# Rerouting the last small output rows of an attention-and-MLP backward kernel away from one DMA engine

## The chip, the cores and the metric

One Trainium2 chip, one core of it. The metric is the device time of one execution in microseconds (us); the profile's own span, from the first to the last instruction of the program, is 1.7 to 1.8 us shorter. The profile counts sixteen DMA engines for the core. A DMA engine takes its packets from several queues: those of the engine that ends last come from q0, q1 and q10 in the trace.

## The reference, cut to what matters

One token goes through a layer norm, attention over a cache of 32 heads x 8192 positions x 128, and a gated MLP. Asked for are the output and the gradients of eight inputs. Almost all of the bytes are the two caches (read once) and their two gradients (written once), each 64 MiB.

```python
def _f(A_x, A_k_cache, A_v_cache, A_wq, A_wo, B_w1, B_w3, B_w2):
    xn = _layernorm(A_x)
    return A_x + attention(xn, A_k_cache, A_v_cache, A_wq, A_wo) + swiglu(xn, B_w1, B_w3, B_w2)
_out, _vjp = jax.vjp(_f, ...)
return (_out, *_vjp(grad_out))   # out_0: 640 values; out_1, the gradient of x: 640 values; out_2, out_3: caches; ...
```

## The kernel before

Each head's keys and values are loaded as tiles of 128 partitions x 16 KiB, overwritten by their gradients, and stored from the same tiles. After the last head come the last weight gradients, then out_0 and out_1.

```python
def store(kind, h):
    t = kv_tiles.pop((kind, h))
    ...
    fifo((dkc if kind == "K" else dvc)[h], t[:])       # SP queue, 2 MB
    free_slots.append(t)
    load_next()
# ... cut: 32 heads ...
outers_a(H - 1)                                        # last V gradient and its store
outers_b(H - 1)                                        # last K gradient and its store
fin_od(NG - 1); fin_pe(NG - 1)
fin_wo(NG - 1)                                         # weight gradient, stored by POOL's queue
for ci in range(NC):
    fin_wq(NG - 1, ci)                                 # the same, after the fifth
# ... cut ...
nc.vector.tensor_copy(row_bf, acc[:, 0:DHALF])
out_0v = out_0.rearrange("a b (e c) -> (a b e) c", e=2)
for e in range(2):
    nc.scalar.dma_start(out_0v[e:e + 1, :], row_bf[64 * e:64 * e + 1, :])
# ... cut: backward of the layer norm, a chain of small operations ...
nc.vector.tensor_copy(fin_bf[:], ps_o[0:NC, 0:P])      # NC = 5 rows of 128
nc.scalar.dma_start(out_1.rearrange("a b (c p) -> (a b c) p", p=P), fin_bf[:])
```

## Time and profile before

| | before |
|---|---|
| median of the first three runs | 732.62 us (732.50 to 733.53) |
| span of the profiled run | 731.1 us |
| moved by DMA | 303.53 MB, mean 415 GB/s |
| last arithmetic ends, span ends | 717.2 us, 731.1 us |
| out_1's last landing, the last kv store's last landing | 722.19 us, 730.10 us |

Two things are to be read here: the DMA engines are full nearly throughout, and the end is 13.9 us in which no compute engine works. The lines that show both stand in the prediction. The queue that carries ACT's transfers, on the page of the kernel before (columns: packets, MB, share of sixteen engines):

```profile
q10 hardware_dynamic: 18, 0.01, 0.0%
```

Eighteen packets are five transfers: each row is one data packet and one semaphore packet, so the two input rows and two out_0 rows make 8, out_1 with its five rows makes 10.

### The profile page before, as it was taken

Reading aid. Unit: us, or ns where it says so; the run is one execution under the profiler, and the core shown is the slowest. Engines: PE = TensorE matmul, PEld = TensorE weight load, DVE = VectorE, ACT = ScalarE, POOL = GpSimd, SP = SyncE. Lnnn points to the kernel's source line nnn. Section 1 sums busy time; section 2 is a strip of 40 time slices with the busy share of each in tenths; the row PEclk is TensorE's granted clock in tenths of the full one; section 3 lists DMA queues with packets and bytes.
Section 4 is the critical chain, followed back from the end, with each engine's and each line's share of the span. In section 5 each row is a group of like instructions: output and inputs, shape, how many; then the busy total and the mean of one; then the engine's idle time right before and its main releaser. Section 6 shows DMA issues by size and latency. Waiting matters only on the chain.

```text
span 731.1 us, 12909 instructions
## 1 busy us (share of the span) xinstructions
PE 602.7 (82%) x5193; PEld 376.1 (51%) x5193; DVE 461.3 (63%) x811; ACT 375.8 (51%) x727; POOL 29.9 (4%) x45
## 2 busy tenths in 40 slices
PE   3989589999999989886987898789697879977930
PEld 2557356665566556554555554455464545544510
DVE  4179646677768886676546765647656775667581
ACT  3640736665666566554554554545464545555510
POOL 0010100000100000001000000000000000000000
PEclk9996799999999999999998999989999999999965
DMA  8999999999999999999999999999999999999993
GB/s 344 403 410 422 424 429 426 418 421 424 422 407 428 428 425 424 425 428 431 423 430 425 431 424 428 427 430 426 426 428 427 430 425 429 429 429 430 430 407 130
DMA packets 27135, 303.53 MB, mean 415 GB/s; under 512 B 2798, under 2 KB 4146, under 8 KB 10434
## 3 DMA queue, kind: packets, MB, share of 16 engines
q1 hardware_dynamic: 21328, 276.39, 89.4%
q0 software_dynamic: 5728, 26.30, 8.9%
q8 instruction: 41, 0.67, 0.4%
q14 instruction: 20, 0.16, 0.1%
q10 hardware_dynamic: 18, 0.01, 0.0%
HBM read 151.34 MB, written 151.34 MB: 414 GB/s over the span
## 4 chain that ended last, share of the span: by engine, by line
DMA 51%; PE 35%; DVE 6%; ACT 3%; issue 1%; SPq 0%; ACTq 0%; DVEq 0%
DMA kv<-in_A_k_cache_dram 22%; DMA out_dram<-kv 17%; PE pT L318 16%; DMA kv<-in_A_v_cache_dram 11%; PE sA L339 4%; PE dA L339 3%; PE X L433 3%; DVE kv L466 3%; PE m L356 2%; DMA wo_g<-in_A_wo_dram 2%; ACT KT L320 1%; ACT kv L630 1%; PE gu_ps L549 1%; PE dh_ps L560 1%; PE dx_acc L648 1%
## 5 line engine op out<-in xcount | busy, mean ns | idle before, releaser
L320 ACT COPY KT<-pT 128x512 f32<-128x512 f32 x512 | 288.0, 587 | 229.5 <-PE pT L318 209.0
L318 PE MATMUL pT<-ident_f,kv 128*128 128x128 f32 x2048 | 308.2, 290 | 60.3 <-DMA kv<-in_A_v_cache_dram 29.5
L318 PEld LDWEIGHTS pT<-ident_f,kv 128*128 128x128 f32 x2048 | 237.1, 149 | 153.7 <-issue 52.2
L466 DVE TENSOR_TENSOR kv<-qd,U 128x4096 bf16<-128x4096 bf16 x64 | 146.1, 2285 | 0.0
L466 DVE TENSOR_TENSOR kv<-qd,P 128x4096 bf16<-128x4096 bf16 x64 | 143.6, 2285 | 0.0
L433 PE MATMUL X<-kv,Z 128*32 128x512 bf16 x1024 | 94.3, 405 | 1.8 <-DVE Z L450 1.8
L339 PE MATMUL sA<-KT,qz 128*32 128x512 bf16 x512 | 83.9, 408 | 0.0
L339 PE MATMUL dA<-KT,qz 128*32 128x512 bf16 x512 | 83.8, 406 | 0.0
L416 DVE SCALAR_TENSOR_TENSOR U<-m,P 128x64 bf16<-128x64 f32 x32 | 7.5, 234 | 82.0 <-PE m L356 82.0
L382 DVE TENSOR_REDUCE mrow<-m 128x1 f32<-128x64 f32 x32 | 7.2, 223 | 75.3 <-PE m L356 75.2
L339 PEld LDWEIGHTS <-qz 128*32 128x32 bf16 x1024 | 29.5, 95 | 40.9 <-issue 38.3
L433 PEld LDWEIGHTS <-Z 128*32 128x32 bf16 x1024 | 32.5, 99 | 34.5 <-issue 6.9
L356 PE MATMUL m<-selc,KT 64*128 64x64 f32 x256 | 30.2, 240 | 8.1 <-ACT KT L346 7.9
L356 PEld LDWEIGHTS m<-selc,KT 64*128 64x128 f32 x256 | 21.3, 142 | 30.1 <-ACT KT L346 21.2
L376 ACT CAST qd<-pT 128x256 bf16<-128x256 f32 x32 | 11.9, 372 | 41.1 <-DVE kv L466 31.6
L389 DVE TENSOR_REDUCE negM<-m 128x1 f32<-128x128 f32 x32 | 9.3, 292 | 33.3 <-PE m L386 33.3
L514 DVE SCALAR_TENSOR_TENSOR wq_g<-wq_g,side 128x512 bf16<-128x512 bf16 x40 | 27.3, 683 | 0.0
L257 DVE SCALAR_TENSOR_TENSOR side<-wo_g,g_bc 128x640 bf16<-128x640 bf16 x32 | 26.2, 820 | 1.1 <-DMA wo_g<-in_A_wo_dram 0.7
L448 DVE SCALAR_TENSOR_TENSOR U<-m,P 128x128 bf16<-128x128 f32 x32 | 11.4, 355 | 15.7 <-PE m L446 15.7
L406 DVE RECIPROCAL rZ<-m 128x1 f32<-128x1 f32 x32 | 5.3, 167 | 24.1 <-PE m L400 24.1
L346 ACT COPY KT<-dA 64x512 f32<-64x512 f32 x32 | 18.6, 583 | 3.1 <-PE dA L339 3.1
L346 ACT COPY KT<-sA 64x512 f32<-64x512 f32 x32 | 18.6, 580 | 2.3 <-PE sA L339 1.9
(161 smaller groups left out, 373.3 us busy)
## 6 DMA issues: line engine op xcount, KB each, us to landing
out_dram<-kv SPq DMA_DIRECT2D x64, 2048.0 KB, 31.0
kv<-in_A_k_cache_dram SPq DMA_DIRECT2D x32, 2048.0 KB, 26.3
kv<-in_A_v_cache_dram SPq DMA_DIRECT2D x32, 2048.0 KB, 26.3
out_dram<-wo_g POOLq DMA_DIRECT2D x8, 640.0 KB, 11.5
out_dram<-wq_g POOLq DMA_DIRECT2D x8, 640.0 KB, 13.3
wq_g<-in_A_wq_dram POOLq DMA_DIRECT2D x7, 640.0 KB, 13.3
wo_g<-in_A_wo_dram POOLq DMA_DIRECT2D x7, 640.0 KB, 19.1
kv<-in_B_w_dram SPq DMA_DIRECT2D x2, 1728.0 KB, 27.9
```

What stands on the lines that cost most here:

```text
L257: nc.vector.scalar_tensor_tensor(junk[:], G_["wo"][:, hh, :], 1.0, g_bc[:], ALU.mult, ALU.mult, accum_out=G_["do"][:, hh:hh + 1])
L318: nc.tensor.transpose(pT[:, k * P:(k + 1) * P], W3[:, 4 * c + k, :], ident_f[:])
L320: nc.scalar.copy(KT[:].rearrange("p k w -> p (k w)"), pT[:])
L339: nc.tensor.matmul(S_[kind][q:q + QW, :], lhsT=S_["qz"][:, o:o + QW], rhs=KTb[c][:, par, :], start=(c0 == 0 and par == 0), stop=(c0 == NCH ...
L346: nc.scalar.copy(XS[0:QH].rearrange("p k w -> p (k w)"), S_.pop(kind)[0:QH, :])
L356: nc.tensor.matmul(S_["m"][:, b0:b0 + 4 * J].rearrange("p (x c k t) -> p k x c t", x=4, k=4, t=2)[:, k], lhsT=XS[0:QH, k, :], rhs=selc[0:Q ...
L376: nc.scalar.copy(qd[:].rearrange("p a d -> p (a d)"), hd[h].pop("ps_r"))
L389: nc.vector.tensor_reduce(S_["negM"][:], S_["m"][:, 2 * J:2 * J + P], AX.X, ALU.max, negate=True)
L433: nc.tensor.matmul(xg["X"][q:q + QW, :], lhsT=Z[:, o:o + QW], rhs=W[:, N4 * i:N4 * (i + 1)], start=(slot == 0 and i < 4), stop=(slot == NS ...
L448: nc.vector.scalar_tensor_tensor(S_["U2"][:], S_["V"][:, 0:J].unsqueeze(2).to_broadcast([P, J, 2]), S_["m"][:, OC + NS:OC + NS + 1], S_["P ...
L466: nc.vector.tensor_tensor(dst[:, lo * DH:hi * DH].rearrange("p (j a b) -> p j a b", a=DH // 2, b=2), vec.rearrange("p (a b) -> p a b", b=2 ...
L514: nc.vector.scalar_tensor_tensor(wq_g[:, ci, :], wq_g[:, ci, :], 1.0, dqb, ALU.mult, ALU.mult, accum_out=dxa[:, ci, g:g + 1])
```

## The change

The intent: DMA engine 4 finishes last, so no late small transfer should need it. Out_0 is to leave in four pieces for each half, out_1 as four rows and one row, all on engines 0 to 3.

```diff
-    out_0v = out_0.rearrange("a b (e c) -> (a b e) c", e=2)
+    out_0v = out_0.rearrange("a b (e q c) -> (a b e) q c", e=2, q=4)
     for e in range(2):
-        nc.scalar.dma_start(out_0v[e:e + 1, :], row_bf[64 * e:64 * e + 1, :])
+        nc.scalar.dma_start(out_0v[e:e + 1], row_bf[64 * e:64 * e + 1, :].rearrange("p (q c) -> p q c", q=4))
 ...
-    nc.scalar.dma_start(out_1.rearrange("a b (c p) -> (a b c) p", p=P), fin_bf[:])
+    for lo, hi in ((0, 4), (4, NC)):
+        nc.scalar.dma_start(out_1.rearrange("a b (c p) -> (a b c) p", p=P)[lo:hi, :], fin_bf[lo:hi, :])
```

## The prediction

> **What bounds the kernel now.** I read the page first: engines, slices, DMA queues, the chain that ended last.
>
> ```profile
> PE 602.7 (82%) x5193; PEld 376.1 (51%) x5193; DVE 461.3 (63%) x811; ACT 375.8 (51%) x727; POOL 29.9 (4%) x45
> ...
> DMA  8999999999999999999999999999999999999993
> GB/s 344 403 410 422 424 429 426 418 421 424 422 407 428 428 425 424 425 428 431 423 430 425 431 424 428 427 430 426 426 428 427 430 425 429 429 429 430 430 407 130
> ...
> DMA 51%; PE 35%; DVE 6%; ACT 3%; issue 1%; SPq 0%; ACTq 0%; DVEq 0%
> ```
>
> No compute engine is full; the DMA engines are at nine tenths or more in every slice but the first and the last, and half of the chain is transfers. The kernel is bound by moving 303.53 MB. The change touches only what happens after the last attention head, so the last slices matter: that slice (18 us) moves only 130 GB/s. Next, the timeline near the end:
>
> ```profile
> 714.85 0.26 ACTq L837 DMA_DIRECT2D out_dram<-KT  x1
> ...
> 716.93 0.28 DVE L853 CAST fin_bf<-pT 5x128 bf16<-5x128 f32 x1 [0.56 <-PE pT L851]
> 717.24 0.27 ACTq L854 DMA_DIRECT2D out_dram<-fin_bf  x1
> ```
>
> "KT" is the row of out_0, "fin_bf" the five rows of out_1. All arithmetic is done at 717.2, yet the span is 731.1. What fills the 13.9 us? The table of stretches (columns: busy time of PE, PEld, DVE, ACT, POOL, then clock, DMA share, GB/s):
>
> ```profile
> 718.00:721.00 3.00, 0.00 (x0) 0.00 (x0) 0.00 (x0) 0.00 (x0) 0.00 (x0) 0.50 0.31 124
> 721.00:730.00 9.00, 0.00 (x0) 0.00 (x0) 0.00 (x0) 0.00 (x0) 0.00 (x0) 0.50 0.06 25
> 730.00:731.10 1.10, 0.00 (x0) 0.00 (x0) 0.00 (x0) 0.00 (x0) 0.00 (x0) 0.50 0.00 0
> ```
>
> For nine microseconds the DMA share is 0.06, one sixteenth: **one** of sixteen DMA engines works alone, at 25 GB/s, and everything waits for it. The packet records of the trace name its work: packets of 16384 B on q1 (the big kv stores issued by SP, 611 to 614 ns each) alternating with 4096 B packets on q0 (the weight-gradient store issued by POOL, 160 ns), each starting as the one before ends, until 729.70. The waits of SP's queue say who is waiting:
>
> ```profile
> SPq L880 <- DMA out_dram<-wq_g: 12.0, 1, 12.0
> SPq L880 <- DMA out_dram<-KT: 9.1, 1, 9.1
> ...
> SPq L880 <- DMA out_dram<-kv: 2.2, 1, 2.2
> ```
>
> L880 is the wait for everything at the program's end. It waits 12.0 us, nominally for wq_g (landed 727.67 in the semaphore records), then for the last kv store (landed 730.10). The 9.1 us on "KT" ends at 716.8, long before.
>
> The landing records also say this is no accident of the end. The sixteenth landing of an SP transfer comes about 0.1 us after the fifteenth until 60 us into the run, 2 to 3 us after it near 300 us, and 11.0 us for the last store (719.07 and 730.10). One engine falls steadily behind. Is it the one that the change avoids? Out_1's five rows answer. Their 256 B packets ran at 717.99, 718.02, 718.07, 718.29 and **720.94**; the fifth sits inside the late engine's unbroken sequence (q1 packet 720.327 to 720.941, this packet 720.937 to 720.955, q0 packet from 720.951). So the late engine is the one carrying a single row of out_1, and I take it to be engine 4.
>
> **What the Trainium skill says.** (1) "DMA: Bandwidth & Descriptors", section "Why a DMA increments its semaphore by 16 and not by 1": a hardware-generated transfer uses the largest k up to 16 that divides both sides' slowest dimension, on the lowest-numbered k engines, and the unused 16 - k counts come at once. The trace agrees on counts: out_1's semaphore moves six times (one early step, five landings; k = 5), each out_0 transfer's twice (k = 1). So out_1 uses engines 0 to 4, and out_0 never used engine 4 before the change. (2) Same page, "Queues, rings and completion order": each engine goes round-robin between its queues, packet by packet. The q1/q0 alternation is that; an added small packet takes its own duration and displaces nothing else. (3) Same page, "Anatomy of one DMA": a completion waits for the write's receipt. Here the last packet ends at 729.70 and the semaphore moves at 730.10, 0.40 us, which the change leaves alone. (4) "Runtime: NRT & Kernel Launch", section "Instruction fetch mechanics": instructions arrive in 16 KiB blocks of 256. Queue q8 shows 41 such packets; PE has 10,386 counted instructions, and 10,386 / 256 = 40.6. I suspect those fetches make one engine late; the change does not touch them.
>
> **The change part by part.**
> *Out_1, fifth row off engine 4.* Removes one 256 B packet and its semaphore write from the late engine. Net cost there, start to next start: 720.937 to 720.951 is 14 ns, 721.717 to 721.723 is 6 ns. Gain: 0.02 us, on the path that sets the end.
> *Out_1, second transfer.* One more issue on ACT, 0.27 us (the L854 row), so about 717.5. It lands by about 719 on an engine that is idle: the four early rows ran within 1.1 us of the issue. The end is at 730.1, so some 11 us of slack hide it.
> *Out_0 in four pieces.* Data and semaphore packets go from 4 to 16 in all, at 9 to 30 ns, spread over four engines and done near 716 to 717: nothing on the path.
> *Semaphores.* Transfers from SP and ACT take eight semaphores in turn (100, 102, 103, 104, 106, 108, 109, 110). The last stores have 104, 106, 108, and ACT's three have 100, 102, 103. A fourth ACT transfer may take 104 and push the stores to 106, 108, 109. Their earlier users landed at 697.45, 702.46 and 707.35, so issues may move from 695.87, 701.77, 706.17 to about 697.5, 702.5, 707.4: later by 0.7 to 1.6 us. But the fifteen faster engines still have older stores to drain then (until 703.1, 708.0 and 712.9), the late one longer still, so no engine runs dry. At the end SP walks its semaphores 59 to 65 ns apart; with the last store one place later in that walk, one step fewer follows it: a gain of 0.06 us.
> Sum: -0.02 -0.06 = -0.08 us, or -0.02 if the semaphores stay. 732.62 - 0.08 = 732.54; I say 732.5.
>
> **The rivals.**
> *Out_1 sets the end.* Then freeing it from the late engine's queue would pay. Its last landing was at 722.19, against about 718.9 for the other four: up to 3.3 us, giving 729.3. Against it: the kv store lands at 730.10, 7.9 us after out_1, from the same engine. Moving the row shortens a wait that was not last.
> *Engine 4 is freed of its backlog.* The whole 9 us would then be to gain, 723. Against it: the backlog is kv and wq_g packets that the change does not move; the row is 256 B of some 225 KB (25 GB/s over 9 us) still owed at 721.
> *A new wait on ACT or an added completion ends last.* If the extra transfer had to reuse the semaphore of the very last kv store, it could issue only after 730.1 and land some 1.2 us later: 734. With eight semaphores in turn it needs one last used by an older store, landed by 707.4, or at worst the one of 695.87, whose landing at 718.42 still leaves 10 us. Unlikely.
> *The late engine's lag itself varies.* It accumulates over the run, so its size, not the change, should dominate any difference seen. The three runs before span 732.50 to 733.53, ten times the expected effect.
>
> **Range and chances.** Center 732.5. Eight in ten: 731.9 to 733.3, which is the spread of before plus a little on both sides. Two per cent is 14.7 us, more than the whole tail of 13.9 us after the last arithmetic, so faster by over 2% is almost excluded (0.005); slower by over 2% needs something outside this reasoning (0.01); within 2% 0.985.
>
> **What would show it right or wrong.** In the changed profile: one engine's share (0.06) in the last nine microseconds again; the kv store's landing last, some 11 us after the other fifteen; SP's closing wait on wq_g and kv as now; two issues on ACT near 717.2 and 717.5; out_1's landings complete by about 720 rather than 722.2; no 256 B packet in the late engine's sequence. If that sequence ends more than 1 us earlier than 729.7 after the start, with the same starting lag, a packet on the small queue costs more than its 14 ns and I mis-sized it. If the last landing is out_1's, a semaphore wait took its place. The prediction fails if the lag is changed by something upstream, such as another placement of instruction fetches.

## The result, and the profile after

The changed kernel took 731.04 us in the median of six runs (730.38 to 733.41), the kernel before 732.56 us in six (730.29 to 733.53). The ratio is 0.9991, with a 95% interval of 0.9971 to 1.0012: the same. Ratios here are the mean time of one kernel's fast runs over that of the other's fast runs of the same rounds, so not quite the ratio of the medians.

The profiled run of the changed kernel was shorter by 1.8 us (span 729.3). Is that the change? First the slices of its page, then its timeline near the end:

```profile
DMA  9999999999999999999999999999999999999994
GB/s 344 398 409 422 427 428 425 400 426 422 416 415 428 429 426 424 428 430 426 424 429 429 430 425 427 425 430 429 423 430 425 429 430 429 428 429 429 429 413 183
...
q10 hardware_dynamic: 18, 0.01, 0.0%
```

```profile
712.72 0.53 ACTq L837 DMA_DIRECT2D out_dram<-KT  x2
...
715.07 0.28 DVE L853 CAST fin_bf<-pT 5x128 bf16<-5x128 f32 x1 [0.56 <-PE pT L851]
715.38 0.56 ACTq L855 DMA_DIRECT2D out_dram<-fin_bf  x2
```

The last arithmetic starts at 715.07 where it started at 716.93, 1.86 us earlier, and out_0, the first of the rerouted transfers, is issued at 712.72 where it was at 714.57, 1.85 us earlier. So the pair's 1.8 us were there before any of the rerouted transfers was issued. From the issue of out_1 to the end are 731.13 - 717.24 = 13.9 us before and 729.27 - 715.38 = 13.9 us after. That the two agree so well is partly luck: in the second profile of the changed kernel (experiment 7) the same stretch takes 12.35 us. Whether the change shortens it must be asked of many runs, not of this pair. There is also a first surprise: queue q10 has 18 packets again. Out_0's four pieces do not exist. Its two issues carry one row of 640 B in both traces; the instruction in the trace already names a single run of 640 B, so the view of four adjoining pieces was merged back before it was issued. Half of the change is no change.

Next the table of stretches after (columns: length; busy time of PE, PEld, DVE, ACT, POOL; clock, DMA share, GB/s) and the closing waits of SP's queue:

```profile
716.00:719.00 3.00, 0.00 (x0) 0.00 (x0) 0.00 (x0) 0.00 (x0) 0.00 (x0) 0.50 0.60 251
719.00:723.00 4.00, 0.00 (x0) 0.00 (x0) 0.00 (x0) 0.00 (x0) 0.00 (x0) 0.50 0.35 145
723.00:728.00 5.00, 0.00 (x0) 0.00 (x0) 0.00 (x0) 0.00 (x0) 0.00 (x0) 0.50 0.06 25
```

```profile
SPq L105 <- DMA out_dram<-kv: 20.4, 3, 11.1
SPq L881 <- DMA out_dram<-wq_g: 11.9, 1, 11.9
SPq L881 <- DMA out_dram<-KT: 7.9, 1, 7.9
SPq L881 <- DMA out_dram<-kv: 2.2, 1, 2.2
```

One engine alone at 25 GB/s again, and the same two last waits of 12 and 2.2 us, on wq_g and the last kv store. The packet records of both traces show what did change in the late engine's sequence (start us, duration ns, queue, bytes):

```
before                              after
720.327  614  q1   16384            719.286  614  q1  16384
720.937   18  q10    256            719.896  160  q0   4096
720.951  159  q0    4096            720.053  614  q1  16384
721.107  614  q1   16384            720.663  160  q0   4096
721.717    9  q10      4            720.820  614  q1  16384
721.723  159  q0    4096            721.430  160  q0   4096
```

The row of out_1 and its semaphore packet are gone; the rest goes on as it did. Out_1 is complete 3.1 us after its first issue (718.52) rather than 4.9 us after it (722.19), but the kv store still lands last, at 728.305.

The three-part wait in the first line is the other visible effect. In the kernel before it read

```profile
SPq L105 <- DMA out_dram<-kv: 7.6, 3, 6.0
```

The fourth ACT transfer took semaphore 104, the last three stores moved on to 106, 108 and 109, and SP now waits for those semaphores' older stores before it issues. No run shows a cost of it (ratio 0.9997 in experiment 7): when the last store was issued at 705.63, the engines had older stores to drain, of which the fifteenth landings came at 710.50 and 716.50.

### The profile page after: what moved, and what is told of

Its sections match the earlier page's. It is cut to its first block, busy times and chain, and to the rows that moved or that the text cites. A ratio compares the mean times of both kernels' runs of the same rounds, so it can differ in the third digit from the quotient of the medians.

```text
span 729.3 us, 12910 instructions
## 1 busy us (share of the span) xinstructions
PE 603.3 (83%) x5193; PEld 376.2 (52%) x5193; DVE 461.1 (63%) x811; ACT 376.1 (52%) x727; POOL 29.9 (4%) x45
## 4 chain that ended last, share of the span: by engine, by line
DMA 48%; PE 38%; DVE 6%; ACT 4%; issue 1%; SPq 0%; ACTq 0%; DVEq 0%
DMA out_dram<-kv 21%; DMA kv<-in_A_k_cache_dram 18%; PE pT L318 18%; DMA kv<-in_A_v_cache_dram 7%; PE sA L339 5%; PE X L433 4%; PE dA L339 4%; DVE kv L466 3%; PE m L356 2%; DMA wo_g<-in_A_wo_dram 2%; ACT KT L320 1%; ACT kv L630 1%; PE gu_ps L549 1%; PE dh_ps L560 1%; PE acc L199 1%
## 5 line engine op out<-in xcount | busy, mean ns | idle before, releaser
L433 PE MATMUL X<-kv,Z 128*32 128x512 bf16 x1024 | 96.9, 413 | 1.8 <-DVE Z L450 1.8
```

What stands on the lines that cost most here:

```text
L433: nc.tensor.matmul(xg["X"][q:q + QW, :], lhsT=Z[:, o:o + QW], rhs=W[:, N4 * i:N4 * (i + 1)], start=(slot == 0 and i < 4), stop=(slot == NS ...
```

## The experiments

Eleven kernels ran. Those of one group ran on the same chip with the same runs of the kernel before, whose median was 731.87 us in the first group, 731.66 in the second and 731.90 in the third.

**1. No rows at all: the bound on any gain.** (First group; outputs 0 and 1 wrong.)

```diff
-    for e in range(2):
-        nc.scalar.dma_start(out_0v[e:e + 1, :], row_bf[64 * e:64 * e + 1, :])
 ...
-    nc.scalar.dma_start(out_1.rearrange("a b (c p) -> (a b c) p", p=P), fin_bf[:])
```

> Neither out_0 nor out_1 is stored (wrong result on purpose): the most that any rearrangement of these transfers can give. Theory (the late DMA engine's backlog of 16 KB kv packets and 4 KB weight-gradient packets sets the end): at most 0.1 us better, ratio to before 0.999 to 1.001, the last kv landing again last and the span ending about 1 us after it. Rival (a row of out_1 in the late engine's queue holds the end up): up to 3.3 us better, ratio about 0.9955.

Measured: 731.55 us, ratio 0.9998 (0.9985 to 1.0011). Even removing all three transfers gives nothing that can be measured. The interval leaves room for a gain of 0.15%, 1.1 us, so no way of sending them can be shown to gain more, and the rival that out_1 holds the end up by 3.3 us is out.

**2. Amplify the suspected cost, first try.** (First group.) The same scratch transfer once with five rows (engines 0 to 4) and once with four (0 to 3).

```diff
+    junk = nc.dram_tensor("junk_dram", [5, 256, 2, P], BF16, kind="Internal").ap()   # or 4
+    nc.scalar.dma_start(junk[:, :, 0, :], fin_bf[0:5, :].unsqueeze(1).to_broadcast([5, 256, P]))
```

> After out_1, one more ACT transfer of five rows by 256 pieces of 256 B to a scratch array: 256 more small packets on each of engines 0 to 4. Theory: if engine 4 is the late one and a small packet costs it its 14 ns, the end moves later by 256 x 0.014 = 3.6 us (ratio about 1.005). Rival A (each small packet costs the late engine a whole turn of the other queues, about 0.77 us): later only by what is not overlapped, more than 10 us. Rival B (small packets fit beside the large ones at no cost, or the late engine is not among 0 to 4): no change, ratio 1.000.

> The same with four rows: 256 more small packets on each of engines 0 to 3, none on engine 4. Theory: these engines have 9 to 11 us of slack at the end, 3.6 us fits in, no change, ratio 0.999 to 1.001. If the late engine is one of 0 to 3: 3.6 us later, like the five-row run. If a fourth or fifth ACT transfer costs something by itself, both runs are later by the same amount.

Measured: 736.21 us, ratio 1.0058 (1.0045 to 1.0071) with five rows; 736.55 us, 1.0063 (1.0048 to 1.0077) with four. The four-row expectation failed, and the pair does not tell the theories apart. The packet records say why: when four or five engines send such pieces together, a piece comes on each only every 53 to 60 ns, not every 14. 256 of them take about 15 us, and in the four-row run the extra transfer itself landed last, 17.0 us after its issue at 716.3. The size was wrong, so I halved it.

**3. The same with 128 pieces.** (Second group; the diff is that of 2 with 128 for 256.)

> Five rows by 128 pieces of 256 B after out_1, half of the earlier number, because in the earlier pair the pieces of four or five engines together came only every 53 to 60 ns and the extra transfer itself ended last in both. Now the early engines are done after about 128 x 0.06 = 7.7 us, by 725. Theory (engine 4 is the late one, 14 ns for each piece when it works alone): the end moves later by 128 x 0.014 = 1.8 us, ratio about 1.0025, and one landing of the extra transfer comes last of all, alone. Rival (the late engine is not among the five): no change, ratio 1.000, all five landings by 725.

> Four rows by 128 pieces: engines 0 to 3 only. Theory: hidden in their slack, all four landings by about 725, the last kv store's landing last as before, ratio 0.999 to 1.001. Rival (the late engine is one of 0 to 3, or an added transfer costs by itself): later by 1.8 us or by as much as the five-row run.

Measured: five rows 734.23 us, ratio 1.0029 (1.0017 to 1.0042); four rows 731.80 us, ratio 0.9995 (0.9982 to 1.0008). Now the pair differs by one row alone, and only the row on the fifth engine costs. SP's closing waits, first of the five-row, then of the four-row run:

```profile
SPq L882 <- DMA out_dram<-wq_g: 12.0, 1, 12.0
...
SPq L882 <- DMA junk_dram<-fin_bf: 4.0, 1, 4.0
```

```profile
SPq L882 <- DMA out_dram<-wq_g: 11.9, 1, 11.9
...
SPq L882 <- DMA out_dram<-kv: 2.2, 1, 2.2
```

In the five-row run the last wait is for the extra transfer, in the four-row run for the kv store as ever. The stretches agree, first five rows, then four:

```profile
721.00:726.00 5.00, 0.00 (x0) 0.00 (x0) 0.00 (x0) 0.00 (x0) 0.00 (x0) 0.50 0.25 62
726.00:729.50 3.50, 0.00 (x0) 0.00 (x0) 0.00 (x0) 0.00 (x0) 0.00 (x0) 0.50 0.07 26
729.50:731.10 1.60, 0.00 (x0) 0.00 (x0) 0.00 (x0) 0.00 (x0) 0.00 (x0) 0.50 0.07 17
```

```profile
721.00:725.00 4.00, 0.00 (x0) 0.00 (x0) 0.00 (x0) 0.00 (x0) 0.00 (x0) 0.50 0.23 58
725.00:728.40 3.40, 0.00 (x0) 0.00 (x0) 0.00 (x0) 0.00 (x0) 0.00 (x0) 0.50 0.06 25
```

In both, four early engines (share 0.25 and 0.23 with the late one) send their pieces beside the backlog; they have landed at 726.4 and 724.9. With five rows the late engine has 116 pieces left when its last large packet has ended at 729.32; they follow 14 ns apart from 729.34 to 730.98, 1.6 us. So the late engine is the one that a five-row transfer uses and a four-row transfer does not, and a small packet costs it the 14 ns of the prediction. One row is worth one of 128 such packets.

**4. Move bulk off the late engine.** (First group.) If its backlog sets the end, then fewer of its large packets should show.

```diff
-        fifo((dkc if kind == "K" else dvc)[h], t[:])
+        dst = (dkc if kind == "K" else dvc)[h]
+        for lo, hi in (((0, 60), (60, P)) if kind == "K" and h == H - 1 else ((0, P),)):
+            fifo(dst[lo:hi], t[lo:hi])
```

> The last kv store (2 MB, 128 rows of 16 KB) is cut into 60 rows (15 engines, four rows each) and 68 rows (4 engines, 17 rows each). Engine 4 then has four packets of 0.611 us instead of eight, engines 0 to 3 have 21. Theory (engine 4 is late and its bulk backlog sets the end): the end comes 4 x 0.611 = 2.4 us earlier, ratio about 0.9967, unless engines 0 to 3, with 13 x 0.611 = 7.9 us more, now end last. Rival (the late engine is one of 0 to 3): 7.9 us later, ratio about 1.011. Rival (bulk does not set the end): no change.

Measured: 734.27 us, ratio 1.0026 (1.0012 to 1.0040), neither the gain nor the full loss. The 68-row transfer's four landings came 17.5 to 23.2 us after its issue at 706.37, the last at 729.54; and 25 packets of 16 KB issued by SP took more than 1.0 us after 703 us of the run, where the kernel before has none. (Earlier in the run such packets occur in every kernel; the one before has 66.) So the helpers became late, and slower for each packet than I had reckoned. The records also settle who ended last. The 60-row transfer, which holds the late engine's part, landed last at 726.98. From 727.5 on one engine works alone until 730.26, and the 68-row transfer's last semaphore packet (729.164) stands in its sequence: it is a helper.

**5. Take bulk away, by rows.** (Second group; output 2 wrong.)

```diff
-        fifo((dkc if kind == "K" else dvc)[h], t[:])
+        n = 64 if kind == "K" and h == H - 1 else P
+        fifo((dkc if kind == "K" else dvc)[h][0:n], t[0:n])
```

> The last kv store sends only its first 64 rows (wrong result on purpose): four packets of 16 KB fewer on every engine. Theory (the backlog of bulk packets on the late engine sets the end): 4 x 0.611 = 2.4 us earlier, ratio about 0.9967. Rival (the end is set by something other than the late engine's bytes, such as a fixed completion or out_1): no change.

Measured: 732.80 us, ratio 1.0009 (0.9995 to 1.0023). The theory's 2.4 us are missing; taken alone, this run speaks against it. But 33 packets of 16 KB took over 1.0 us after 703 us of the run, and the V store before it landed 25.4 us after its issue, against 22.9 in the kernel before. In the packet records, four large packets in a row on what I take for the late engine took 1.16, 1.27, 1.28 and 1.34 us between 706.4 and 711.5, where 0.611 each is usual: 5.05 - 2.44 = 2.6 us lost. The new suspicion: a transfer of 64 rows makes two engines read from the same group of partitions, and both slow down.

**6. Three runs on that suspicion.** (Third group.) Half of each row in place of half of the rows; all bytes in two column halves; all bytes in two row halves.

```diff
+        dst = (dkc if kind == "K" else dvc)[h]
+        # last K store:  dst[:, 0:4096]                          half of each row (wrong on purpose)
+        #            or  dst[:, 0:4096], then dst[:, 4096:8192]  cut by columns
+        #            or  dst[0:64], then dst[64:128]             cut by rows
```

> The last kv store sends half of every row, 128 rows of 8 KB (wrong result on purpose). The 64-row run had saved four packets, but [...]four of the late engine's packets took 1.16 to 1.34 us in place of 0.611, 2.6 us lost, which ate the gain of 2.4.[...] Theory (the late engine's bulk bytes set the end, and contention for partitions hid it): 8 x 0.305 = 2.4 us earlier, ratio about 0.9967, late engine's packets of 0.61 us and less. Rival (bytes of the last store do not set the end): no change again.

> The last kv store in two transfers of half rows, the same bytes in all. Theory: eight more semaphore-free packets of the same bytes, one more issue, same end, ratio 0.999 to 1.001. Rival (a second transfer or shorter packets cost by themselves): later.

> The last kv store in two transfers of 64 rows, the same bytes in all. Theory of contention: in the first half two engines read each group of partitions, among them the late engine's while it works off older stores; four of its packets take about 1.27 in place of 0.611 us, so the end is 2.6 us later, ratio about 1.0036. Rival (the 64-row run failed to gain because bulk bytes do not matter): no change, ratio 1.000.

Measured:

| | median us | ratio to before |
|---|---|---|
| half of each row | 729.98 | 0.9971 (0.9959 to 0.9983) |
| all, cut by columns | 732.01 | 0.9999 (0.9987 to 1.0011) |
| all, cut by rows | 735.73 | 1.0049 (1.0037 to 1.0061) |

The first is about the 2.4 us that the theory asked for (0.0029 x 731.9 = 2.1 us; the interval gives 1.2 to 3.0). It takes bytes from all engines, but the trace still shows one of them alone before the end, and the store's sixteenth landing 6.3 us after its fifteenth (726.11 and 719.81):

```profile
720.50:725.70 5.20, 0.00 (x0) 0.00 (x0) 0.00 (x0) 0.00 (x0) 0.00 (x0) 0.50 0.06 24
```

Together: **bytes on the late engine set the end**. The second and third move the same bytes in the same number of transfers and differ only in the direction of the cut, by 0.5%. The stretch from 706.4 to 715 shows the difference, cut by columns, then cut by rows:

```profile
706.40:715.00 8.60, 1.81 (x12) 0.88 (x12) 7.27 (x25) 0.59 (x1) 1.05 (x2) 0.50 0.98 405
```

```profile
706.40:715.00 8.60, 1.80 (x11) 1.00 (x10) 7.16 (x26) 0.59 (x1) 1.63 (x2) 0.50 1.00 326
```

The engines are equally busy, at shares of 0.98 and 1.00, but move 405 GB/s in one and 326 in the other: the same work takes them longer. 16 KB packets over 1.0 us after 703 us of the run: 1 in the column cut, 49 in the row cut (the column cut's own packets are 8 KB, the longest of them 0.45 us). The loss was 3.6 us rather than the 2.6 expected, so the size is not fully accounted for. That it is the shared partitions is a reading that fits, and it is not shown: the traces do not say which partitions an engine reads. The two cuts also differ in which addresses in memory are written at the same time, and no run separates the two.

**7. The changed kernel once more.** (Second group, no edit.)

> The changed kernel again, beside more runs of the kernel before. Theory: 0.02 us of packets and 0.06 us of closing waits less, nothing that times can show: ratio 0.9985 to 1.0015. Rival (the 1.5 us between the medians of the first comparison is real): ratio 0.998 or below with an interval that leaves out 1.

Measured: 731.79 us, ratio 0.9997 (0.9984 to 1.0009). The 1.5 us between the first medians did not come back.

I found no version that beats both kernels. Only the run that left bytes out (wrong) shortened the end; of the cuts that send them all, none did.

## Why the prediction was right

The prediction said "within 2%" at 0.985, and the ratio is 1 within a fifth of a per cent, twice. Its number is not confirmed: 731.04 and, again, 731.79 us both lie below its range of eight in ten, 731.9 to 733.3. That range was the spread of three runs of the kernel before, and it was too narrow and too high: six runs of that same kernel span 730.29 to 733.53, and its medians in the three later groups are 731.66 to 731.90. The miss is one of the range, not of the mechanism, and the forecast gain of 0.08 us is too small for these times to confirm. Point by point:

- *One late engine sets the end, and out_1's fifth row is on it.* Right. The 128-piece pair identifies the engine; the half-row run, with one engine again alone at the end, shows that bulk bytes carry the end.
- *14 + 6 ns for the row.* The 14 ns are confirmed by 116 packets in a row, of one queue; between packets of other queues they were read once, in the trace of the kernel before. The 6 ns were not measured again.
- *The second transfer hides in slack.* Right: issues at 715.38 and 715.68 (0.26 us each), all landed by 718.5.
- *Out_0's packets go from 4 to 16.* **Wrong**: I took the diff's four pieces at their word. They were merged into one; the count stayed at 4. It cost nothing only because nothing there is on the path.
- *Semaphores.* Right: 104 for the new transfer, 106, 108, 109 for the stores. In the closing walk SP takes one more step after the wait for the last kv store where it took two, so the drain begins 0.14 us after that landing (728.448 - 728.305) and not 0.20 us (730.302 - 730.099): the 0.06 us are in the trace, though no time can show them.
- *The lag varies more than the change is worth.* Right, and the profile pair is a warning: 1.8 us between the two spans, all of it accrued before out_0 was issued. Even the gap between the last store's fifteenth and sixteenth landing was 11.0 us before and 5.6 after, where six landings came between 720.4 and 722.8, ahead of the last.
- *The rivals.* "Out_1 sets the end" falls by the run without rows. "A new wait on ACT or an added completion ends last" did not happen in the changed kernel, but it did in the 256-piece runs, which shows how it looks.

Open: why this engine falls behind over the run. The suspicion of the prediction, instruction fetches, was not tested; the change does not depend on it.

## What to carry to other kernels

When the end of a kernel is one DMA engine working off a backlog, ask how many bytes of that backlog a change moves: a 256-byte row among some 225 KB is worth its own 14 ns, whatever its landing time suggests. A transfer that lands late is not the one that ends the kernel unless its landing is the last. To size such a thing, remove it altogether for the bound, then amplify it with a twin that differs in one engine only. And if you cut a transfer, try the cut by columns before the cut by rows: here the first cost nothing and the second 3.6 us, for a reason that stays open.

## What the Trainium skill lacked or had wrong

- "DMA: Bandwidth & Descriptors", section "Latency and other measured facts", says that engines 7 and 15 are usually the slow ones. Here the late engine is used by a five-row transfer and not by a four-row one, so by the page's own rule on k (the lowest-numbered k engines) it is engine 4; its landing of the last store came 11.0 us after the fifteenth in the kernel before.
- The same page, section "Rules for kernel authors", says of two transfers to disjoint partition halves that they serialize and are not worth it. Here they were worse than that: cut by rows the store cost 3.6 us (ratio 1.0049), with 49 packets of 16 KB over 1.0 us in place of 0.611 and 326 GB/s at full DMA share, while cut by columns it cost nothing (0.9999). "SBUF — State Buffer" treats the bandwidth of half of the partitions too, so the lack is not of a warning but of what one such store costs among others in flight.
- No page says that a view of a contiguous row in four adjoining pieces may reach the chip as one run: out_0 had one 640 B packet for each half with and without it (18 packets on the queue in both; the issuing instruction in the trace names one run of 640 B).
